# Halves of 64 rows in the first three steps of a gated attention and maxout kernel, and w_out eight rows to a partition

## The chip, the cores and the metric

The kernel runs on one core of a Trainium2 chip. The metric is the device time of one execution in microseconds. A core has TensorE (matmul; its weight loads are shown apart, as PEld), VectorE (DVE), ScalarE (ACT), GpSimd (POOL), SyncE (SP), and 16 DMA engines that the queues share. [...]

## The reference

Eight sequences of 3072 tokens go through attention without softmax, gated by u, and then through a layer that takes the larger of two projections:

```python
scores = (1.0 / S) * np.matmul(z, z.transpose(0, 2, 1))     # z: 8 x 3072 x 64
attn = np.maximum(scores, 0.0) ** 2
x = (u * np.matmul(attn, v)).reshape(B * S, D)              # u, v: 8 x 3072 x 256
g = np.maximum(x @ w1, x @ w2)                              # w1, w2: 256 x 1024
out = g @ w_out                                             # w_out: 1024 x 256
```

## The kernel before

A step is 512 tokens of one sequence (a group of four blocks of 128): 8 sequences of 6 steps, 48 steps. In step n a tile of scores (two blocks of rows by the 512 tokens) is a pair of products over 64 rows, one on each half of the array; relu takes it out of PSUM into a_sb, square makes it attn. Scores are symmetric, so a tile is computed once and turned by a transposing DMA on SyncE's queue (aT) for the step that needs the other side.

Attention times v goes two ways. From step 3 on a fast scheme with seven products in place of eight is used: halves of 64 rows and 256 columns named Xa, Xb, Ya, Yb, with sums on VectorE (es) and folded values of v (lf). The first three steps (PLAIN = 3) multiply plainly: a product of v's block over all 128 rows into each of two banks, acc0 and acc1, for each of the 24 blocks of rows (add_plain, L859). A first or last part of such a step takes four blocks for one bank and then for the other, so that a bank comes free early.

The second layer runs two to three steps behind. The maximum is computed as x(w1 - w2) through relu plus x w2 w_out, so w2 is transposed on TensorE once (w2t, L1593) and multiplied by w_out (w2o). The first-layer products are named d, in four units of two blocks of 512 columns; each unit has a first part a and a second part b (a0 b0 a1 a2 b1 b2 a3 b3), in which the two halves of the array work on different banks and then change over. The w_out products use the seven-product scheme too in steps 3 to 46; their four parts are s0 to s3 here. In a step the order is s0 a0 s1 b0 Xa s2 Xb a1 a2 s3 b1 b2 Ya (a3 in it) b3 Yb.

Where two parts change over between halves and banks, a fence keeps them apart: an empty instruction on GpSimd's queue waits for the last product before (mark, L93), and the next product waits for it (fence, L87). POOL's queue also issues the loads of v, u, z and the weights; a timed load waits for a product of TensorE (load, L106).

The order of TensorE's work is written out: a list of work with planned times, into which groups of score tiles ("windows", L1400) are laid at certain spots (L1461 to L1475). Everything else (which of ScalarE and VectorE does a tile, the order of each queue, which buffer a tile takes) is dealt by a planner that runs the list through costs and due times (find_orders, L1779) and keeps the best of 24 rounds. The DMA dictionary (L206) and FIRST_LOADS (L209) are its guesses of transfers; at_step(b, s, us) names the job of TensorE at a planned time in a step, and fixes when a load is requested.

The weights of the second layer come in with these layouts (L1580): w1 and w2 as "(c p) f -> p c f", w_out as "(c p) d -> p c d", row c x 128 + p of w_out in partition p, 1024 pieces of one row.

Of the kernel before, what the change touches and what calls it, by code (L numbers as in the profile page):

```python
# [11 lines left out]
def kernel(  # L12
# [45 lines left out]
    W2O_AT, A3_AT = 0, 4  # L58
# [47 lines left out]
    def load(timed=False, **kw):  # L106
        dma = pin(nc.gpsimd.dma_start(**kw))
# [98 lines left out]
    DMA = dict(turn=1180, uT=1130, zT=4220, store=1940, v=1680, u=1680, z=3130, w1=4100, w2=3000, wo=4500)  # L206
    DMA_SMALL, DMA_PART, DMA_FULL, DMA_FULL_TO = 970, 0.9, 1.1, 100000
    DMA_START, DMA_END, DMA_LATE, DMA_AHEAD, SP_ISSUE = {"SP": 870, "POOL": 1770}, 1330, 4000, 4500, 1450
    FIRST_LOADS = {("v", 0, 0): 0, ("v", 0, 1): 1200, ("v", 0, 2): 2500, ("v", 0, 3): 3700, ("v", 0, 4): 4900, ("v", 0, 5): 7700, ("u", 0): 6300}  # L209
# [209 lines left out]
    def add_pair(st, k0, head=None):  # L419
# [19 lines left out]
        def do_square(eng):  # L439
# [4 lines left out]
            RELU,  # L444
# [414 lines left out]
    def add_plain(st, keyed, ks, dcs):  # L859
        first = [st.count[dc] == 0 for dc in dcs]  # L860
        counts = []
        for k in ks:
            counts.append(st.count[dcs[0]])
            for dc in dcs:
                st.count[dc] += 1
        accs = [(f"acc{dc}", st.n) for dc in dcs]
        new = [a for a, f in zip(accs, first) if f]
        for pool, key in new:
            acc_buf(int(pool[-1]), key)

        def fn(_):
            for k, n in zip(ks, counts):
                for dc in dcs:
# [3 lines left out]
                        a_rows(st, k - k % 2)[:, k % 2],  # L877
# [5 lines left out]
        key = ("plain", st.n, keyed)  # L883
        for g in groups:
# [3 lines left out]
            {"PE": PE512 * len(ks) * len(dcs)},  # L888
# [184 lines left out]
    def add_second(st, split):  # L1073
# [17 lines left out]
        for i in range(KF // 2):  # L1091
# [23 lines left out]
            def halves_of(part, i=i, bank=bank):  # L1115
                if part:
                    fence.append(marks.pop(("d", n, i)))
                for kc in range(KD):
                    for half in range(2):
# [4 lines left out]
                            w1_sb[:, kc, ts(2 * i + j, P)],  # L1124
# [180 lines left out]
    plain_todo = []  # L1305

    for n, st in enumerate(steps):
# [57 lines left out]
        def put_plain(ks, dcs, reads):  # L1365
            global_i = len(plain_todo)
            i = sum(t[0] is st for t in plain_todo)
            plain_todo.append((st, i, ks, dcs))
            put(PE512 * len(ks) * len(dcs), False, ("plain", st.n, i), reads)

        for i, k0 in enumerate(own):
            if i in ((0, 1) if n else ()) + (len(own) - 2, len(own) - 1):
                if i in (0, len(own) - 2):
                    ks = [own[i], own[i] + 1, own[i + 1], own[i + 1] + 1]
                    for dc in range(KD):
                        put_plain(ks, [dc], [((n, own[i]), lat), ((n, own[i + 1]), lat)])
                continue
            for k in (k0, k0 + 1):
                put_plain([k], range(KD), [((n, k0), lat)])
# [21 lines left out]
    for i, (n, k0) in enumerate(tiles):  # L1401
# [13 lines left out]
        if tiles[i + 1 : i + 2] and tiles[i + 1][0] // NG > n // NG:  # L1415
            room = 0

# [43 lines left out]
    spots = [i for i, at in enumerate(begins) if free(i) and apart(at) and not work[i][1]]  # L1461
# [3 lines left out]
    for w in reversed(range(len(windows))):  # L1465
        limit = min([limit] + [due[r] for r in windows[w] if r in due])
        found = [i for i in spots if begins[i] <= limit]
        i = found[-1] if found else 0
# [4 lines left out]
    laid = {i: [w for w in ws if w > 6] for i, ws in laid.items()}  # L1473
    for w, i in ((2, 2), (3, 5), (4, 8), (5, 11), (6, 14)):
# [84 lines left out]
    for n in range(len(steps)):  # L1559
# [91 lines left out]
    for args in plain_todo:  # L1651
        st, i, ks, dcs = args
        add_plain(st, i, ks, list(dcs))
# [59 lines left out]
    for key, before in zip(pe_order, [None] + pe_order):  # L1713
        if key[0] == "score" and (before is None or before[0] == "plain"):
# [288 lines left out]
```

## Time and profile before

| | |
|---|---|
| median of 3 runs | 893.06 us (890.72 to 893.35) |
| profiled execution | 893.2 us, span 891.4 us, mean granted clock 0.998 |
| TensorE busy | 882.7 us of the span (99%) |
| VectorE, ScalarE busy | 802.4 us (90%), 757.9 us (85%) |
| GpSimd busy | 59.8 us (7%) |
| packets' time in SyncE's DMA queue (hardware), in GpSimd's (software) | 79.3% and 23.3% of the 16 engines' span |
| steps 0, 1, 2 on TensorE | products from 7.69 us, from 23.82, from 37.60; w2t at 50.45 |

The span is the time from the first to the last instruction of the profiled execution; the rest of its time lies around it. A busy TensorE is not one at its peak: matmuls are pipelined, their ends are modelled, and a gap of 0.1 us between two kinds of product does not show as idle. In the views a row gives the start, the length of the whole group, engine, line, operation, tiles, and the count; the idle time before it and what ended it stand in brackets.

### The profile page before, as it was taken

How to read it: one execution, taken by the hardware profiler on the slowest of the kernel's cores; microseconds unless marked ns; L12 is line 12 of the kernel's file. 1: busy time of each engine (PE TensorE's matmuls, PEld its weight loads, DVE VectorE, ACT ScalarE, POOL GpSimd, SP SyncE). 2: the span in 40 equal slices, each digit the busy share in tenths (PEclk: the TensorE clock that was granted, in tenths of full speed). 3: DMA queues.
4: the chain of work that ended last, by engine and by line, in shares of the span. 5: the costliest groups of instructions: out<-in, count | busy, mean ns of one | idle time of the engine just before them, and what ended most of it. 6: DMA issues, size and time to landing. Idle time of an engine off the chain costs nothing.

```text
span 891.4 us, 37531 instructions
## 1 busy us (share of the span) xinstructions
PE 882.7 (99%) x16501; PEld 738.0 (83%) x16501; DVE 802.4 (90%) x1720; ACT 757.9 (85%) x952; POOL 59.8 (7%) x127
## 2 busy tenths in 40 slices
PE   9999999999999999999999999999999999999998
PEld 3368888878889988888888878888888898888886
DVE  6867799989999999999999999989998999989985
ACT  8867998879988999789997899978999799997634
POOL 3100000000000000000000000000000010000000
PEclk9999999999999999999999999999999999999999
DMA  9999999999999989999899999999999999996722
GB/s 160 171 167 148 188 199 160 179 188 187 157 163 169 193 151 174 170 179 203 121 169 173 191 184 143 169 166 213 150 148 172 187 199 158 136 199 115 128 58 73
DMA packets 380853, 146.17 MB, mean 164 GB/s; under 512 B 359184, under 2 KB 360848, under 8 KB 380688
## 3 DMA queue, kind: packets, MB, share of 16 engines
q1 hardware_dynamic: 364128, 114.01, 79.3%
q0 software_dynamic: 16560, 29.74, 23.3%
q8 instruction: 129, 2.11, 1.0%
q14 instruction: 36, 0.29, 0.1%
HBM read 59.77 MB, written 25.17 MB: 95 GB/s over the span
## 4 chain that ended last, share of the span: by engine, by line
PE 93%; ACT 3%; DMA 1%; DVE 1%; issue 1%; POOL 0%
PE acc L86 48%; PE s_ps L86 46%; ACT a_sb L282 1%; DMA aT<-a_sb 1%; ACT g_sb L282 1%; ACT o_sb L282 0%; DMA o_sb<-in_z_dram 0%; ACT g_last L282 0%; DVE gs L299 0%; DVE gs L296 0%; ACT a_sb L288 0%; ACT w2T_sb L293 0%; PE w2t_ps L1593 0%; DVE e L296 0%; DVE a_sb L290 0%
## 5 line engine op out<-in xcount | busy, mean ns | idle before, releaser
L86 PEld LDWEIGHTS <-v_sb 64*128 64x128 bf16 (+1 forms) x4464 | 332.4, 94 | 62.2 <-issue 8.4
L282 ACT ACTIVATE a_sb<-s_ps 128x1024 bf16<-128x1024 f32 (+1 forms) x335 | 302.3, 941 | 36.5 <-PE s_ps L86 33.6
L86 PEld LDWEIGHTS <-lf 64*128 64x128 bf16 x3240 | 264.2, 94 | 16.2 <-POOLq L94 3.2
L86 PE MATMUL acc<-es,v_sb 64*128 64x256 bf16 x2160 | 274.9, 269 | 0.0
L86 PE MATMUL acc<-es,lf 64*128 64x256 bf16 x1080 | 245.0, 269 | 0.0
L86 PE MATMUL acc<-a_sb,lf 64*128 64x256 bf16 x1224 | 232.1, 269 | 0.0
L86 PE MATMUL s_ps<-xT,w_sb 64*128 64x512 bf16 (+1 forms) x1504 | 212.6, 376 | 0.1
L288 ACT ACTIVATE a_sb<-a_sb 128x1024 bf16<-128x1024 bf16 (+1 forms) x224 | 209.9, 966 | 1.5
L282 ACT ACTIVATE g_sb<-s_ps 128x1024 bf16<-128x1024 f32 x187 | 186.0, 1024 | 14.0 <-PE s_ps L86 12.0
L86 PE MATMUL acc<-aT,lf 64*128 64x256 bf16 x936 | 177.5, 269 | 2.0 <-DMA aT<-a_sb 2.0
L86 PE MATMUL acc<-a_sb,v_sb 64*128 64x256 bf16 (+1 forms) x1344 | 140.2, 279 | 0.4 <-DVE xT L303 0.2
L86 PE MATMUL s_ps<-zT 64*128 64x512 bf16 (+2 forms) x774 | 120.2, 334 | 1.0 <-DVE zT L130 0.4
L86 PEld LDWEIGHTS <-gs 64*128 64x128 bf16 x2816 | 103.3, 94 | 9.9 <-issue 0.7
L296 DVE TENSOR_TENSOR es<-aT 128x1536 bf16<-128x1536 bf16 (+1 forms) x117 | 106.2, 931 | 0.5
L86 PEld LDWEIGHTS <-w_sb 64*128 64x128 bf16 (+1 forms) x1520 | 78.2, 94 | 25.5 <-POOLq L94 1.5
L86 PEld LDWEIGHTS <-g_sb 64*128 64x128 bf16 x2304 | 87.7, 94 | 10.4 <-POOLq L94 7.3
L290 DVE TENSOR_TENSOR a_sb<-a_sb 128x1024 bf16<-128x1024 bf16 (+1 forms) x112 | 72.2, 648 | 22.7 <-ACT a_sb L282 22.6
L86 PE MATMUL acc<-aT,v_sb 64*128 64x256 bf16 x936 | 86.8, 270 | 0.0
L299 DVE TENSOR_TENSOR es<-a_sb 128x512 bf16<-128x512 bf16 x198 | 79.4, 419 | 8.2 <-PE acc L86 8.0
L86 PE MATMUL s_ps<-wf_sb,gs 64*128 64x128 bf16 x2112 | 85.6, 217 | 0.0
L296 DVE TENSOR_TENSOR es<-a_sb 128x1024 bf16<-128x1024 bf16 x108 | 72.7, 684 | 0.0
L86 PE MATMUL s_ps<-w_out_sb,g_sb 64*128 64x128 bf16 (+1 forms) x1600 | 72.6, 222 | 0.0
(94 smaller groups left out, 1101.4 us busy)
## 6 DMA issues: line engine op xcount, KB each, us to landing
out_dram<-o_sb SPq DMA_DIRECT2D x47, 512.0 KB, 4.9
v_sb<-in_v_dram POOLq DMA_DIRECT2D x48, 256.0 KB, 5.8
u_sb<-in_u_dram POOLq DMA_DIRECT2D x48, 256.0 KB, 5.0
aT<-a_sb SPq DMA_TRANSPOSE x228, 5.1
z_sb<-in_z_dram POOLq DMA_DIRECT2D x7, 384.0 KB, 6.3
w_sb<-in_moe_w_dram POOLq DMA_DIRECT2D x2, 512.0 KB, 6.7
uT<-u_sb SPq DMA_TRANSPOSE x48, 5.2
a_sb<-a_sb SPq DMA_TRANSPOSE x45, 5.6
```

Of the source, the lines that this page charges most:

```text
L86: newest[0] = pin(nc.tensor.matmul(*args, **kw)).ins
L282: pin(nc.scalar.activation(out_ap, in_ap, AF.Relu))
L288: pin(nc.scalar.activation(ap, ap, AF.Square))
L290: pin(nc.vector.tensor_mul(ap, ap, ap))
L296: pin(nc.vector.tensor_add(*args))
L299: pin(nc.vector.tensor_sub(*args))
```

## The change

In step 0 all but the last two tiles' products, and in steps 1 and 2 those of tiles 3 to 8 of 12, are made of half-row products: in mode A the lower half of v's block goes to acc0 while the upper half of it, for the other 128 columns, goes to acc1; in mode B the two change over. Six runs of step 0 alternate between the modes; steps 1 and 2 have one run of A and one of B between full products (mode F). At each change of mode there is a fence. The score windows of step 1 and the first of step 2 are grouped anew, and laid between the runs. The planner no longer counts a passage for scores beside halves.

w_out is read as "(p c) d -> p c d", eight rows in one piece for each partition. Row 8 p + c now lies in partition p, so the first layer takes every eighth column of w1 and w2 as a block: by_place gives that view, and it is used in the weights of all d products and in w2's transposes. The request times of some loads, guesses of DMA times and the order of two first loads (u of step 0 before the last two groups of v) change with it.

```diff
-    W2O_AT, A3_AT = 0, 4
+    W2O_AT, A3_AT = 1, 4
...
+    def by_place(tile_sb):
+        return tile_sb.rearrange("p c (q n) -> p c n q", n=KF)
...
-    DMA = dict(..., wo=4500)
+    DMA = dict(..., wo=3000)
-    FIRST_LOADS = {..., ("v", 0, 4): 4900, ("v", 0, 5): 7700, ("u", 0): 6300}
+    FIRST_LOADS = {..., ("v", 0, 4): 6300, ("v", 0, 5): 7700, ("u", 0): 4900, ("uT", 0): 12000}
...
-            RELU,
+            {"DVE": RELU["DVE"]} if (n, k0) == (1, 6) else RELU,
...
-    def add_plain(st, keyed, ks, dcs):
+    def add_plain(st, keyed, ks, dcs, mode):
...
-                st.count[dc] += 1
+                st.count[dc] += 1 if mode in "AB" else 2
...
+        key = ("plain", st.n, keyed)
+        before, after = (plain_modes.get(("plain", st.n, keyed + i)) for i in (-1, 1))
+        waits, marked = before not in (None, mode), after not in (None, mode)
 
         def fn(_):
+            if waits:
+                fence.append(marks.pop(("plain", st.n)))
             for k, n in zip(ks, counts):
+                moving = a_rows(st, k - k % 2)[:, k % 2]
+                if mode in "AB":
+                    for half in range(2):
+                        dc = half ^ "AB".index(mode)
+                        halved(
+                            half,
+                            tile_of(f"acc{dc}", st.n),
+                            v_tile(st.b, k // G)[:, k % G, ts(dc, P)],
+                            moving,
+                            start=n == 0,
+                            stop=n == 2 * NSB - 1,
+                        )
+                    continue
                 for dc in dcs:
                     matmul(
...
-                        stop=(n == NSB - 1),
+                        stop=(n == 2 * NSB - 2),
                     )
+            if marked:
+                marks["plain", st.n] = mark()
...
-                            w1_sb[:, kc, ts(2 * i + j, P)],
+                            by_place(w1_sb)[:, kc, 2 * i + j, :],
...
+    FIRST_RUNS = [("A", 0, 2), ("B", 0, 3), ("A", 2, 5), ("B", 3, 6), ("A", 5, 10), ("B", 6, 10)]
...
+        if n == 0:
+            for run in FIRST_RUNS:
+                first_windows.append(len(work))
+                put_halves(*run)
+            first_windows.append(len(work))
+            put_banks(10)
+        else:
+            put_banks(0)
+            put_whole(2)
+            put_halves("A", 3, 9)
+            put_halves("B", 3, 9)
+            put_whole(9)
+            put_banks(10)
...
+    windows[6:11] = [[(1, k0) for k0 in ks] for ks in ((0, 2), (4, 6, 8), (10, 12, 14), (16, 18, 20), (22,))] + [[(2, 0), (2, 2)], [(2, 4)]]
...
-    laid = {i: [w for w in ws if w > 6] for i, ws in laid.items()}
-    for w, i in ((2, 2), (3, 5), (4, 8), (5, 11), (6, 14)):
+    laid = {i: [w for w in ws if w > 7] for i, ws in laid.items()}
+    laid = {i: [w for w in ws if w not in (9, 10, 11, 12)] for i, ws in laid.items()}
+    for w, i in [*zip(range(2, 8), first_windows[1:]), (9, first_windows[-1] + 6), (10, first_windows[-1] + 8), (11, first_windows[-1] + 12), (12, first_windows[-1] + 15)]:
...
-            add_u(n, quiet(at_step(pb, ps, 2 if pb == 0 and ps < LAG else 1), ("Xa",)))
+            add_u(n, quiet(at_step(pb, ps, (2 if ps == 0 else 2.3) if pb == 0 and ps < LAG else 1), ("Xa",)))
...
-            v_at = [(0, 8), (3, 9), (4, 4), (4, 9), (5, 4), (5, 9)]
+            v_at = [(0, 8.7), (3, 9), (4, 4), (4, 9), (5, 4), (5, 9)]
...
-        (lambda: tile_of(*W2), moe_w2, "w2", (0, 7), W2, "(c p) f -> p c f"),
-        (lambda: w1_sb, moe_w1, "w1", (1, 2), None, "(c p) f -> p c f"),
-        (lambda: w_out_sb, moe_w_out, "wo", (2, 2), None, "(c p) d -> p c d"),
+        (lambda: tile_of(*W2), moe_w2, "w2", (0, 6.9), W2, "(c p) f -> p c f"),
+        (lambda: w1_sb, moe_w1, "w1", (1, 2.3), None, "(c p) f -> p c f"),
+        (lambda: w_out_sb, moe_w_out, "wo", (2, 2.3), None, "(p c) d -> p c d"),
...
-                pin(nc.tensor.transpose(tile_of("mm", ("w2t", 0))[:, dc, nb, :], tile_of(*W2)[:, dc, ts(nb, P)], ident))
+                pin(nc.tensor.transpose(tile_of("mm", ("w2t", 0))[:, dc, nb, :], by_place(tile_of(*W2))[:, dc, nb, :], ident))
...
-        if key[0] == "score" and (before is None or before[0] == "plain"):
+        if key[0] == "score" and (before is None or plain_modes.get(before) == "F"):
             jobs[key].ways = {"PE": jobs[key].ways["PE"] + 2 * SWITCH}
...
-                j.done = dma_free[0] + (DMA_LATE if begin > 125000 and j.key[0] != "zT" else DMA_END)
+                j.done = dma_free[0] + (DMA_LATE + 1500 * (j.key[0] == "v") if begin > 125000 and j.key[0] != "zT" else DMA_END)
...
-    early_loads = [("v", 0, g) for g in range(NG - 1)] + [("u", 0), ("v", 0, NG - 1)]
+    early_loads = [("v", 0, g) for g in range(NG - 2)] + [("u", 0), ("v", 0, NG - 2), ("v", 0, NG - 1)]
```

More of the change, by code (lines that the diff above doesn't have):

```diff
@@ L887, in add_plain @@
             key,
-            {"PE": PE512 * len(ks) * len(dcs)},
+            {"PE": PE512 * len(ks) * len(dcs) // (2 if mode in "AB" else 1)},
             fn,
@@ L1123, in halves_of @@
                             bank(j),
-                            w1_sb[:, kc, ts(2 * i + j, P)],
+                            by_place(w1_sb)[:, kc, 2 * i + j, :],
                             tile_of(*xT)[:, :, kc, :],
@@ L1363, with put_plain, rows_at, put_halves @@
         n_plain = 0
-        def put_plain(ks, dcs, reads):
-            global_i = len(plain_todo)
+        def put_plain(mode, ks, dcs, reads):
             i = sum(t[0] is st for t in plain_todo)
[L1368 to L1379, printed above, removed]
+            plain_todo.append((st, i, ks, dcs, mode))
+            plain_modes["plain", st.n, i] = mode
+            ns = PE512 * len(ks) * len(dcs) // (2 if mode in "AB" else 1)
+            put(ns, False, ("plain", st.n, i), reads)
+        def rows_at(i):
+            return [((n, own[i]), lat)]
+        def put_halves(mode, first, end):
+            for i in range(first, end):
+                put_plain(mode, [own[i], own[i] + 1], range(KD), rows_at(i))
+        def put_whole(i):
+            for k in (own[i], own[i] + 1):
+                put_plain("F", [k], range(KD), rows_at(i))
+        def put_banks(i):
+            ks = [own[i], own[i] + 1, own[i + 1], own[i + 1] + 1]
+            for dc in range(KD):
+                put_plain("F", ks, [dc], rows_at(i) + rows_at(i + 1))
+        if n == 0:
[11 more added lines that the diff above has]
+            put_banks(10)
     assert LAG == 3
@@ L1459, in apart @@
         return n >= LAG or (at - starts[n]) % (6 * 432) == 0
-    spots = [i for i, at in enumerate(begins) if free(i) and apart(at) and not work[i][1]]
+    spots = [i for i, at in enumerate(begins) if free(i) and apart(at) and not work[i][1] and at >= starts[1]]
     GAP_FIRST, GAP, GAP_LATER = 2100, 600, 1200
@@ L1651 @@
     for args in plain_todo:
-        st, i, ks, dcs = args
-        add_plain(st, i, ks, list(dcs))
+        st, i, ks, dcs, mode = args
+        add_plain(st, i, ks, list(dcs), mode)
     for b in range(B):
```

11 lines of the change are left out of this document (5 added, 6 removed).

## The prediction

> **What bounds the kernel now.** First the page: which engine is busy, and what the chain that ended last consists of.
>
> ```profile
> PE 882.7 (99%) x16501; PEld 738.0 (83%) x16501; DVE 802.4 (90%) x1720; ACT 757.9 (85%) x952; POOL 59.8 (7%) x127
> PE 93%; ACT 3%; DMA 1%; DVE 1%; issue 1%; POOL 0%
> ```
>
> TensorE is busy 882.7 of 891.4 us and makes 93% of the chain. So an edit pays in two ways only: TensorE's own work gets shorter, or one of the few gaps of TensorE closes. The view of the waits, for TensorE, names one gap of weight, and the chain in order of time gives its place and what it costs.
>
> ```profile
> PE acc L86 <- DMA aT<-a_sb: 2.0, 1, 2.0
> ```
> ```profile
> 131.31 2.12 PE s_ps L86 x64
> 182.68 8.27 DMA aT<-a_sb
> 242.81 2.12 PE s_ps L86 x64
> 350.71 2.12 PE s_ps L86 x64
> 458.42 2.12 PE s_ps L86 x64
> ```
>
> The same place of the loop comes round every six steps. From 242.81 to 350.71 it takes 107.9 us, to 458.42 another 107.7; but from 131.31 to 242.81 it takes 111.5. That one round loses 3.7 us, and in it lies the only step of the chain that is a transfer: a transposing DMA into aT, issued at 182.68, on which TensorE waits until about 190.95. The wait is 2.0 us, so 1.7 us of the 3.7 are something else. The busy time by short stretches (columns: stretch, length, then busy time of PE, PEld, DVE, ACT, POOL, then PEclk, DMA share, GB/s) shows what:
>
> ```profile
> 190.00:192.00 2.00, 1.01 (x20) 0.91 (x21) 2.00 (x4) 0.47 (x1) 0.00 (x0) 0.94 0.99 194
> 192.00:194.00 2.00, 2.00 (x40) 1.97 (x37) 1.96 (x5) 1.61 (x2) 0.00 (x0) 0.50 1.23 265
> 194.00:196.00 2.00, 2.00 (x28) 1.66 (x26) 0.00 (x0) 1.01 (x2) 0.53 (x1) 0.70 1.67 340
> ```
>
> Behind the wait the granted clock is 0.94, 0.50 and 0.70: 2 x (0.06 + 0.50 + 0.30) = 1.7 us of full-speed work lost. So this one late transfer costs 2.0 + 1.7 = 3.7 us. [...]
>
> Why is that transfer late? SyncE's queue at the same place of two rounds:
>
> ```profile
> 153.48 13.19 SPq L103 DMA_TRANSPOSE aT<-a_sb  x6
> 182.68 5.71 SPq L103 DMA_TRANSPOSE aT<-a_sb  x2
> 257.53 15.23 SPq L103 DMA_TRANSPOSE aT<-a_sb  x6
> 288.60 4.15 SPq L103 DMA_TRANSPOSE aT<-a_sb  x2
> ```
>
> The places lie 111.5 us apart on TensorE. 257.53 - 111.5 = 146.0, so the first round issues its six transposes 7.5 us later than the second one; at 288.60 - 111.5 = 177.1 it is still 5.6 us late. It is a backlog, and it is being worked off. It began where the DMA engines went from idle to full; the busy tenths of the DMA engines in the stretch 38 to 52 us (40 slices of 0.35 us), and then in 50 to 190:
>
> ```profile
> DMA  0000000499947938999999999999999999999962
> ```
> ```profile
> DMA  9999999989999989999999999999999999999999
> ```
>
> Idle from 38 to 40.5, busy ever after, up to the wait. The w_out load is the first of that flood.
>
> **The change part by part.** *Halves.* A pair of half-row products, one on each half of the array, takes the place of one full product; there are as many pairs as there were products, so the streaming itself gains nothing. What goes is the cost of passing between full-row products and score products, which are halves already. TensorE's rows in step 1:
>
> ```profile
> 26.50 0.82 PE L86 MATMUL s_ps<-zT 64*128 64x512 bf16 x6
> 27.25 2.76 PE L86 MATMUL acc<-a_sb,v_sb 128*128 128x512 bf16 x12
> 29.95 0.82 PE L86 MATMUL s_ps<-zT 64*128 64x512 bf16 x6
> ```
>
> One period is 29.95 - 26.50 = 3.45 us. Twelve products, at (2.76 - 0.38) / 11 = 0.216 each, are 2.59; six score halves, two at a time, are 0.65. The rest, 0.21 us, is two passages: 0.105 each. Before the change there are 14 groups of scores among products, 6 in step 0 and 4 each in steps 1 and 2, so 28 passages. In the changed order I count: step 0 runs in halves up to its last two tiles, which leaves 1 passage; step 1 has a group at its start (2), one where halves begin (1), one where they end (1), and the rest stand among halves; step 2 the same 4. That is 9. W2O_AT = 1 moves the full-row w2o products behind the first group of step 3's halves, 2 more. 28 - 11 = 17 passages, 1.8 us gained.
>
> Against it stands the beginning of step 0:
>
> ```profile
> 7.69 1.02 PE L86 MATMUL acc<-a_sb,v_sb 128*128 128x512 bf16 x4
> 8.39 1.28 DVE L290 TENSOR_TENSOR a_sb<-a_sb 128x1024 bf16<-128x1024 bf16 x2
> 8.65 0.61 PE L86 MATMUL s_ps<-zT 64*128 64x512 bf16 x4
> 9.18 0.11 PEld L86 LDWEIGHTS <-v_sb 128*128 128x128 bf16 x2 [0.42 <-issue]
> ```
>
> Now four full products (0.86) and a group of scores lie between 7.69 and 9.18, and the square of the second tile, the first of VectorE's two from 8.39, is ready about 9.05. In mode A the first tile gives only 0.43 us of products, and the scores come behind the second tile: TensorE is out of work at 8.12 and waits until about 9.15, 1.0 us. Step 3 thus starts about 1.8 - 1.0 = 0.8 us earlier. ScalarE's relus of step 0 get their scores up to 0.9 us later at first; by my dealing none of the later groups waits for them. If that cover is gone, 0.9 us is the price.
>
> *Fences.* Each change of mode is a wait of TensorE on a GpSimd instruction that itself waits for the last product before: 6 in step 0, 3 in each of steps 1 and 2. An existing fence, with the loads of the weights around it:
>
> ```profile
> 185.44 0.24 PE L86 MATMUL s_ps<-xf_sb,xT 64*128 64x128 bf16 x2
> 185.45 0.17 PEld L86 LDWEIGHTS <-w_sb 64*128 64x128 bf16 x4
> 185.50 0.61 PE L86 MATMUL s_ps<-xT,w_sb 64*128 64x512 bf16 x4
> 185.79 0.37 PEld L86 LDWEIGHTS <-g_sb 64*128 64x128 bf16 x8 [0.17 <-POOLq L94]
> 185.93 0.40 PE L86 MATMUL s_ps<-w_out_sb,g_sb 64*128 64x128 bf16 x8
> 186.16 0.28 PEld L86 LDWEIGHTS <-g_sb 64*128 64x128 bf16 x8
> 186.21 0.40 PE L86 MATMUL s_ps<-w_out_sb,g_sb 64*128 64x128 bf16 x8
> ```
>
> The last product ends at 185.68 and the fenced weights load at 185.79: 0.11 us, hidden behind four halves (0.43 us). In the changed order two or three tiles' scores (0.43 to 0.65 us) stand in every such place; a product's tail of 0.16 beyond its slot, 0.11 and the load's lead of about 0.1 make 0.37. I take nothing, margin 0.06. Behind the fence on GpSimd's queue only its load issues wait; the moved times (6.9, 8.7, 2.3) place each load after a fence, not ahead of it. A load issue in front would cost up to its own length:
>
> ```profile
> 40.67 0.92 POOL L107 DMA_DIRECT2D w_out_sb<-in_moe_w_out_dram  x1 [12.55 <-PE acc L86]
> ```
>
> Seven loads lie in these steps, so 0 to 6 us; I take 0.
>
> *Loads.* The w_out load goes from 1024 pieces of a row to 128 of eight rows. Time from issue to landing:
>
> ```profile
> w_sb<-in_moe_w_dram POOLq DMA_DIRECT2D x2, 512.0 KB, 6.7
> w_out_sb<-in_moe_w_out_dram POOLq DMA_DIRECT2D x1, 512.0 KB, 8.5
> ```
>
> The nearest row for the same bytes in larger pieces is w_sb's 6.7: up to 1.8 us less of a full queue, or nothing; I take 0.9. It is requested 0.4 us later in the step, which starts 0.8 earlier. So the flood ends 0.4 + 0.9 = 1.3 us earlier, and TensorE reaches the late aT 0.8 us earlier: the wait of 2.0 becomes about 1.5, bounds 0.6 to 2.4. The dealing of all later work is computed anew, so this transfer may also stand elsewhere in its queue; the rounds behind show no wait at all.
>
> *w1 by place.* All first-layer products now take weights whose columns lie eight elements apart, 1504 matmuls, and the 16 transposes of w2 as well. No row of this trace has such a load. Cost from below 0, from above in the rival. I take 0, because the nearest row, w_sb's 4 loads in 0.17, leaves room: (0.17 - 0.09) / 3 = 27 ns each, 54 ns for the two of a pair that streams 216.
>
> **The sum.** The profiled execution took 893.2 us (its span 891.4 and 1.8 around it), 0.1 over the median of 893.06. Less 0.8 for steps 0 to 2. If the wait is gone: less 3.7 more, 888.7. If it is still 1.5 but too short for the clock to drop: the flood's end decides, 893.2 - 1.3 - 1.7 = 890.2. My forecast is between, **889.5 us**.
>
> **The rivals.** *The wait stays and drops the clock.* Then only the flood's end counts: 893.2 - 1.3 = 891.9, or 893.2 if w_out's form saves nothing and the first part's gain is all given back as waiting. For it: the backlog is DMA's, and 2.0 us of wait has once been enough. Against: the dealing is new. The runs before, 890.72 to 893.35, spread by 2.6 us, less than the 3.7 of wait and drop together but more than the drop alone, so it may not come each time.
>
> *Slower: the spaced weights load slowly.* Where products of 128 columns run, eight and the two of xT behind them, five pairs, go from 185.93 to 186.21: 56 ns a pair, hardly more than its two loads take (eight in 0.28: (0.28 - 0.09) / 7 = 27 ns each, 54 a pair). If a spaced load took twice as long, the two would take 107 ns, and the first pair behind such a stream would start its second half 107 - 54 = 53 ns late, in three places of a step: a0 behind s0, b0 behind s1, b1 behind s3. 3 x 44 steps x 53 ns = 7.0 us: 893.2 - 3.7 + 7.0 = 896.5, or 899.4 with the wait staying. It decides from 27 ns upward; at four times (107 ns each) the three places lose 160 ns, 21 us, and beyond that the pairs of 512 columns themselves. The row that would be spaced:
>
> ```profile
> L86 PEld LDWEIGHTS <-w_sb x1520: 92/94/98, 51.3 to 880.2; 64*128 64x128 bf16 x188, 128*128 128x128 bf16 x2
> ```
>
> [...] No row of before can settle this.
>
> *A new wait.* The new dealing puts another operand late, once, with the clock's drop: 893.2 - 0.8 + 3.7 = 896.1 if the old wait stays too, 892.4 if it only moves. *The halves don't run side by side*: spoken against by the score halves above, six in three slots.
>
> **How the numbers follow.** Forecast 0.50; the wait stays (or only moves) 0.30; spaced weights 0.13; a second wait 0.07. A measurement of this kernel tells about 0.3%, 2.7 us, from no change, so faster means under 890.4 and slower over 895.7. The forecast is nearly all below 890.4, the wait that stays lies in between, the last two above: faster 0.48, same 0.33, slower 0.19. The range goes from 887.5 (the wait gone, w_out's full 1.8, some of the passages' margin) to 896.5, which takes in a second wait and the lower price of spaced weights. The first two cases alone hold 887.5 to 893.5.
>
> **What would show it.** Right: 0.43 us of products at 7.7, a wait of 1.0, then score rows without a gap of 0.1 on each side up to the last tiles of step 0; w2t's transposes about 0.8 us before 50.4; no row of PE waiting on aT, or one under 1.5 us, with the clock at 1.00 in every stretch; the first round at 107.8 us. Wrong: LDWEIGHTS of w_sb over 100 ns, or gaps at the first product of a first-layer unit in every round, which would lift the later rounds above 107.7; PE waiting on GpSimd's queue in the first 50 us; a clock of 0.50 anywhere.

## The result, and the profile after

The changed kernel takes 898.15 us in the median of 12 executions (892.89 to 906.15), the kernel before 893.11 beside it (890.67 to 899.14): the ratio is 1.0060, 95% interval 1.0032 to 1.0087. (Here and below the ratios leave out executions more than 1.5% above the fastest of their kernel; the medians hold all.) The prediction of 889.5 us, and its range up to 896.5, missed: it is slower. The profiled execution took 903.62 us, its span 901.9; that of before 893.2.

The page after, its first line on the engines and the chain that ended last:

```profile
PE 885.6 (98%) x16589; PEld 765.5 (85%) x16589; DVE 801.3 (89%) x1720; ACT 758.5 (84%) x952; POOL 59.4 (7%) x127
PE 92%; DMA 3%; ACT 2%; DVE 2%; issue 1%; POOL 0%; SPq 0%; POOLq 0%; ACTq 0%; DVEq 0%
```

TensorE still bounds, but DMA's share of the chain has gone from 1% to 3%. The beginning came out as forecast. TensorE's rows of step 0, and a weight load behind a fence (columns: start, length, and in brackets the wait ahead of it):

```profile
7.84 0.59 PE L86 MATMUL acc<-a_sb,v_sb 64*128 64x512 bf16 x4
9.45 0.61 PE L86 MATMUL acc<-a_sb,v_sb 64*128 64x512 bf16 x4 [1.01 <-DVE a_sb L293]
10.31 0.61 PE L86 MATMUL acc<-a_sb,v_sb 64*128 64x512 bf16 x4
```
```profile
10.16 0.26 PEld L86 LDWEIGHTS <-v_sb 64*128 64x128 bf16 x4 [0.17 <-POOLq L94]
```
```profile
L1640 PE MATMUL w2t_ps<-ident,w_sb x16: 219/225/230, 49.1 to 50.0; 128*128 128x128 bf16 x16
```

Four half-row products take 0.59 to 0.61 us, where four over all rows took 1.02 at the same place in the kernel before: the two halves run side by side. The wait of 1.01 us is there. The weight load waits 0.17 us for the fence at 10.16, but the product it serves starts at 10.31 without a wait. From the first product of step 0 to w2's transposes it is 49.1 - 7.84 = 41.3 us, against 50.45 - 7.69 = 42.8 before: 1.5 us gained, where 0.8 was forecast. And no wait for aT is left at 189 us. But TensorE's waits now read:

```profile
PE acc L86 <- DMA aT<-a_sb: 3.4, 1, 3.4
PE acc L86 <- DMA a_sb<-a_sb: 1.7, 1, 1.7
PE acc L86 <- DVE a_sb L293: 1.0, 1, 1.0
```

The first two stand in step 3, a few microseconds after the gained 1.5. TensorE's rows there, and the busy time in stretches of 2 us with the granted clock (the number after POOL's):

```profile
57.25 0.38 PE L86 MATMUL acc<-aT,v_sb 64*128 64x256 bf16 x4
61.07 0.29 PE L86 MATMUL acc<-aT,lf 64*128 64x256 bf16 x2 [3.43 <-DMA aT<-a_sb]
63.11 0.58 PE L86 MATMUL acc<-a_sb,v_sb 64*128 64x256 bf16 x3 [1.67 <-DMA a_sb<-a_sb]
```
```profile
62.00:64.00 2.00, 0.89 (x10) 0.72 (x11) 2.00 (x5) 0.00 (x0) 0.00 (x0) 0.50 0.97 78
64.00:66.00 2.00, 2.00 (x22) 1.61 (x20) 1.93 (x6) 0.00 (x0) 0.00 (x0) 0.50 1.27 167
68.00:70.00 2.00, 2.00 (x33) 1.83 (x31) 0.36 (x2) 0.36 (x1) 0.00 (x0) 0.81 0.96 104
```

Two waits, and half clock from 61.93 us for 6.83 us by the trace's record of the clock, so it begins within the second wait. Adding 3.43 + 1.67 + 3.4 = 8.5 us counts a part of that wait twice. Measured between equal places of TensorE, against the run zearly_after below, which has the same order and no stop, it costs 8.3 us (72.88 against 64.32, less the 0.30 by which it was later already). The two profiled executions differ by 10.4 us: 8.3 from here, less 1.5 at the start, less the 3.7 of the old gap at 189 us, and 3.4 from the rounds of six steps, each of which takes 0.45 us longer (below). Of the 3.9 left, 1.4 are waits for ScalarE and VectorE in the round behind the stop, 1.3 are waits for nothing visible (at 313 and 381 us), and 1.2 stay unassigned.

One wait in one profile isn't a median. The mean granted clock of each execution tells how often clock is lost, though not where: 0.998 means about 3.6 us at half clock (0.002 x 2 x 893). Of 24 executions of the changed kernel (12, and 12 in a second run) 13 show 0.998 or less, with a median of 902.4 us; the other 11 have a median of 896.8. Of 145 executions of the kernel before, run beside the kernels below, 28 show it (median 898.5), and the other 117 have a median of 893.3. I call them **executions with lost clock** below. In the changed kernel they are more frequent, 54% against 19%, and its other executions are slower too, by 3.5 us; the rounds less the gain at the start explain 1.9 of these.

### The profile page after: what moved, and what is told of

It is laid out like the page before. It is cut to its first block, busy times and chain, and to the rows that moved or that the text cites. A ratio compares the mean times of both kernels' runs of the same rounds, so it can differ in the third digit from the quotient of the medians.

```text
span 901.9 us, 37712 instructions
## 1 busy us (share of the span) xinstructions
PE 885.6 (98%) x16589; PEld 765.5 (85%) x16589; DVE 801.3 (89%) x1720; ACT 758.5 (84%) x952; POOL 59.4 (7%) x127
## 4 chain that ended last, share of the span: by engine, by line
PE 92%; DMA 3%; ACT 2%; DVE 2%; issue 1%; POOL 0%; SPq 0%; POOLq 0%; ACTq 0%; DVEq 0%
PE acc L86 47%; PE s_ps L86 44%; DMA a_sb<-a_sb 2%; ACT g_sb L285 1%; DMA z_sb<-in_z_dram 1%; DMA aT<-a_sb 0%; ACT a_sb L285 0%; ACT a_sb L291 0%; DVE es L299 0%; DVE a_sb L293 0%; DVE es L302 0%; DVE o_sb L299 0%; DVE zT L133 0%; DVE gs L302 0%; DVE e L299 0%
## 5 line engine op out<-in xcount | busy, mean ns | idle before, releaser
L86 PEld LDWEIGHTS <-v_sb 64*128 64x128 bf16 x4552 | 334.6, 94 | 61.5 <-issue 10.0
L86 PE MATMUL s_ps<-xT,w_sb 64*128 64x512 bf16 (+1 forms) x1504 | 215.9, 378 | 0.5 <-ACT g_sb L285 0.4
L291 ACT ACTIVATE a_sb<-a_sb 128x1024 bf16<-128x1024 bf16 x225 | 210.9, 966 | 1.5
L86 PE MATMUL acc<-a_sb,v_sb 64*128 64x256 bf16 (+2 forms) x1424 | 142.0, 284 | 3.9 <-DMA a_sb<-a_sb 1.7
L86 PE MATMUL s_ps<-zT 64*128 64x512 bf16 (+2 forms) x774 | 122.4, 333 | 1.8 <-ACT o_sb L296 0.7
L86 PEld LDWEIGHTS <-w_sb 64*128 64x128 bf16 (+1 forms) x1520 | 105.8, 142 | 14.0 <-issue 1.2
L86 PEld LDWEIGHTS <-g_sb 64*128 64x128 bf16 x2304 | 91.1, 95 | 8.5
L86 PE MATMUL s_ps<-w_out_sb,g_sb 64*128 64x128 bf16 (+1 forms) x1600 | 76.8, 226 | 0.0
```

Source lines behind the costliest of these rows:

```text
L86: newest[0] = pin(nc.tensor.matmul(*args, **kw)).ins
L291: pin(nc.scalar.activation(ap, ap, AF.Square))
```

## Which part of the change: the parts alone

*The spaced weights and the layout of w_out, without halves.* Edits to the kernel before; layout_only has both lines, spaced_only the first (its rows of w_out then meet other columns of the first layer, so it computes another sum by the same instructions):

```diff
-    w1_sb[:, kc, ts(2 * i + j, P)]
+    by_place(w1_sb)[:, kc, 2 * i + j, :]      # and in w2's transposes
-    (lambda: w_out_sb, moe_w_out, "wo", (2, 2), None, "(c p) d -> p c d"),
+    (lambda: w_out_sb, moe_w_out, "wo", (2, 2), None, "(p c) d -> p c d"),
```

> The kernel before with the spaced weights of w1 and w2 alone (w_out's rows then meet other columns of the first layer than in the reference); no halves, w_out in pieces of one row, the order as before. Theory S: weights loads of w_sb 141 ns, 108.2 us a round, so 893.1 + 2.9 = 896. If the round's longer time came from the halves' dealing instead: 107.8 us a round and 893.1.

> The kernel before with w_out in eight rows to a partition and the spaced weights; no halves, the order as before. Theory S: 896 less what the wide load brings in the backlog, up to 1.3 us: 894.7 to 896. Theory W: the wide pieces hold up the turns, a wait on a transfer between 50 and 65 us or a longer one at 189: 897 to 900.

*The halves, without the spaced weights.* Edits to the changed kernel: contiguous columns in by_place, and for halves_only also the old layout of w_out, so that halves_wide keeps its wide rows (and computes another sum too):

```diff
-    return tile_sb.rearrange("p c (q n) -> p c n q", n=KF)
+    return tile_sb.rearrange("p c (n q) -> p c n q", n=KF)
```

> The changed kernel with w_out read as before (one row to a piece) and contiguous weights of w1 and w2; halves, score windows, request times and the whole dealing stay. Theory S (spaced weights cost in every round, the halves' schedule makes the early waits): the round of six steps comes back from 108.2 to 107.8 us, weights loads of w_sb 94 ns, w2t at about 49.1 us, and the waits on transfers between 50 and 65 us stay in some executions: median about 895 (898.15 less 2.9). Theory W (the wide pieces of w_out hold up the turning transfers in the DMA engines): the early waits are gone too, and the median is 889 to 891.

> The changed kernel with contiguous weights of w1 and w2 (each partition's rows of w_out then meet other columns of the first layer than in the reference); w_out still in 128 pieces of eight rows. Beside the changed kernel it takes away the spaced loads alone. Theory S: 108.2 to 107.8 us a round, 2.9 us less in all, about 895, early waits as in the changed kernel. Theory W: the same 2.9 us less, early waits as in the changed kernel; against halves_only it is slower by the early waits, 3 to 6 us.

Measured (12 executions each, ratio to before with its interval):

| kernel | median us | ratio | with lost clock | clean round of six steps |
|---|---|---|---|---|
| spaced_only | 894.24 | 1.0021 (0.9993 to 1.0049) | 3 | 107.83 |
| layout_only | 895.06 | 1.0012 (0.9982 to 1.0041) | 3 | 107.83 |
| halves_only | 901.36 | 1.0050 (1.0019 to 1.0080) | 10 | 108.05 |
| halves_wide | 895.21 | 1.0021 (0.9989 to 1.0053) | 3 | 108.05 |

A clean round is the time between two equal places of TensorE six steps apart, with no wait in it; before it is 107.71, in the changed kernel 108.16. So the spaced weights cost 0.12 us a round, 0.9 us over 7.5 rounds, and the other 0.33, 2.5 us, come with the rest of the change, though no halves are left after step 2. Theory S, which put all of it down to the weights, is out. The load that was in dispute:

```profile
L86 PEld LDWEIGHTS <-w_sb x1520: 137/141/168, 50.0 to 890.2; 64*128 64x128 bf16 x188, 128*128 128x128 bf16 x2
```

141 ns against 94: half as much again, nearly all of it behind running products. halves_only, with w_out in 1024 pieces, stops in step 3 as well (1.3 us for aT, 0.9 for a_sb<-a_sb): the wide rows are not what holds the turnings up, and theory W is out too. halves_only and halves_wide differ in w_out's layout alone and lose clock in 10 and in 3 of 12 executions; no run shows why, and a share of twelve executions is a coarse number.

## What holds up the turnings of step 3: the load of z

SyncE's queue at that place, and the load of the next sequence's z on GpSimd's queue; then z's time from issue to landing, after and before:

```profile
39.60 8.48 SPq L103 DMA_TRANSPOSE aT<-a_sb  x3
48.18 1.50 SPq L103 DMA_TRANSPOSE a_sb<-a_sb  x1
```
```profile
45.17 0.53 POOL L107 DMA_DIRECT2D z_sb<-in_z_dram  x1 [3.64 <-ACT a_sb L285]
```
```profile
DMA to landing us min/median/max: 15.8/15.8/15.8
```
```profile
DMA to landing us min/median/max: 9.7/9.7/9.7
```

z is requested at 45.17 and lands at 60.97. The third of the three turnings of aT, requested at 42.33, lands at 61.02, and that of a_sb at 63.06, as the chain in order of time has it:

```profile
48.18 14.88 DMA a_sb<-a_sb
```

In the kernel before the turning of a_sb is issued at 46.21 and takes 10.2 us, so it lands at 56.4, and z at 56.2:

```profile
46.21 1.21 SPq L103 DMA_TRANSPOSE a_sb<-a_sb  x1
```

In the changed kernel TensorE goes on at 61.07 and 63.11. While they are under way the DMA engines are busy but move 60 GB/s, against 154 before; the row of 50 to 60 us (last numbers: DMA share, GB/s), before and after:

```profile
50.00:60.00 10.00, 9.90 (x105) 6.73 (x105) 9.68 (x25) 6.71 (x9) 0.53 (x1) 1.00 1.36 154
```
```profile
50.00:60.00 10.00, 7.54 (x65) 5.04 (x64) 2.93 (x7) 5.46 (x8) 0.53 (x1) 1.00 1.28 60
```

The trace shows that both kinds slow down together: z, with 15.8 us against 9.7 in the kernel before, and the third turning land within 0.05 us, and the turnings' packets of 256 bytes that begin between 50 and 58 us take 135 ns in the mean, against 32 in the kernel before.

*z later,* in the changed kernel, in halves_only and in the kernel before:

```diff
-    z_at, zT_at = (2, 6), (3, 2)
+    z_at, zT_at = (3, 6), (4, 2)
```

> The changed kernel with the second sequence's z requested one step later (behind the load of u of step 4, about 63 instead of 45 us; its turning moved from step 3 to step 4). Theory Z (the turns that step 3 reads share the DMA engines with z's load and land only when it does): no wait on a transfer between 50 and 65 us, the transfers in 50 to 60 us back to about 150 GB/s, median 893 to 895 instead of 898.15. Theory Q (the halves' order brings one turn more into the queue by 42 us, and the queue is late whatever is beside it): the wait stays, 897 to 899.

> halves_only (w_out in pieces of one row, contiguous weights) with z requested one step later. Theory Z: the waits between 50 and 65 us go, median 892 to 894 instead of 901.4, and faster than the same kernel with the other layout by the 0.9 us of the spaced weights. Theory Q: 899 to 901.

> The kernel before with z requested one step later. It has no wait at 50 to 65 us to lose, but its later backlog shrinks or not: theory Z gives no change there, 893 to 894, or the wait at 189 us goes in more executions, 891 to 893; a z load that disturbs the turns at 63 us instead would show as waits at 65 to 80 us, 895 and more.

Measured: 903.65, 905.94 and 906.57 us (ratios 1.0114, 1.0132, 1.0143; 6, 5 and 4 executions). The wait of step 3 is gone in zlate_after and zlate_halves, as theory Z says (the first d product of step 1 comes at 64.1 us in zlate_after, 72.6 in the changed kernel); zlate_before had none to lose. In all three another wait has come, from about 80 us on, where step 6 needs zT; in zlate_after:

```profile
PE s_ps L86 <- DMA zT<-z_sb: 8.0, 1, 8.0
```

The move was too far, and each kernel is slower for it, where 3 to 9 us less, or no change in the kernel before, were expected.

*z earlier,* in the place of one load of v (in the kernel before 8 stands for 8.7):

```diff
-    z_at, zT_at = (2, 6), (3, 2)
-    v_at = [(0, 8.7), (3, 9), (4, 4), (4, 9), (5, 4), (5, 9)]
+    z_at, zT_at = (0, 8.7), (3, 2)
+    v_at = [(3, 6), (3, 9), (4, 4), (4, 9), (5, 4), (5, 9)]
```

> The changed kernel with contiguous weight loads and the old w_out layout; the request for the second sequence's z moves from about 45 us (step 2) to about 22 us (step 0), in the place of one v request, which moves to step 3. Theory Z (the z load shares the DMA engines with the turnings and u/uT loads that step 3's d products read, so that all land only when z lands, at about 61 us): with z landed before 40 us, the turn of aT that is requested at about 42 us lands within 10 us instead of 18.7, no transfer wait over 1 us between 50 and 70 us and none for zT at 80 us, no stretch of granted clock 0.5 there; bytes moved at 50 to 60 us at 120 GB/s or more; profiled span about 888 to 890 us, time 890 to 892. Theory Q (the early waits come from the order in which the turnings are requested: one turn more stands in the queue at 42 us, whatever else is loaded): the aT wait of 1 to 3 us at 57 to 61 us stays, 892 to 896.

> The changed kernel whole, with z asked for at about 22 us instead of 45, as in the run with contiguous weights. Theory Z: the waits of 3.4 and 1.7 us and the half clock from 61.9 us for 6.8 us go, about 3.4 + 1.7 + 3.4 = 8.5 us in the profiled execution; what is left of the change is the gain ahead of w2's transposes of 1.5 us, the gap of before at 189 us (3.7 us) if it is gone, less 0.45 us a round of six steps (0.33 dealing, 0.12 spaced weights) over 7.5 rounds, 3.4 us: time 891 to 893. Theory Q: the waits stay, 896 to 900.

> The kernel before with z asked for at about 22 us instead of 46, in the place of one v request. It tells whether the gap at 189 us and the early shares of DMA belong to the load of z at all. Theory Z: z shared the engines with the turnings there too but landed by 56 us, ahead of their use, so there is little to gain: same within 0.3%, 891 to 893; the wait at 189 us stays (it depends on requests made long after) or goes by chance of the backlog. Theory Q: no change either, within 0.3%.

Measured: zearly_halves 895.45 us (ratio 1.0015, 0.9985 to 1.0044), zearly_after 900.16 (1.0034, 0.9999 to 1.0068), zearly_before 895.76 (1.0035, 1.0001 to 1.0068). No wait in step 3 in any of the three profiles and none for zT; 50 to 60 us in zearly_after:

```profile
50.00:60.00 10.00, 9.90 (x112) 7.34 (x112) 9.76 (x27) 5.33 (x7) 0.53 (x1) 1.00 1.02 176
```

The profiled execution of zearly_after took 892.34 us, 11.3 less than that of the changed kernel. But the medians did not follow: 7 of 12 executions still lose clock, and 6 of 12 in each of the other two, zearly_before too. So the wait was taken away and the frequency was not. zearly_before is the warning here: neither it nor the kernel before has a wait in step 3, and with z moved it loses clock in 6 of 12, against 5 of 35 of the kernel before beside it. Moving z, and a load of v to step 3 in exchange, may cost clock of its own, so these runs can't tell how much of the changed kernel's lost clock goes with z. To see more executions, I ran both once more, unchanged:

> The changed kernel once more, for a second profile and for twelve more executions with their granted clocks. Theory T (the loss comes from executions in which step 3 waits for its turnings at about 57 to 63 us and the clock then halves): about half of the executions show a granted clock of 0.998 or less, with a median near 901.5, the others near 894; if the profiled execution is one of the disturbed, the wait for aT or a_sb lies between 50 and 70 us. Rival L (waits anywhere, by chance): the same share, but the profile of a disturbed execution shows its wait elsewhere, as a wait for nothing visible or for a transfer after 70 us.

> The changed kernel with z asked for at about 22 us once more. Theory Z (the load of z is what holds up step 3's turnings): no transfer wait between 50 and 70 us in the profile; if this execution is disturbed, its wait lies elsewhere (a wait for nothing visible, or a transfer later), and so the disturbed share stays at about half. Rival: the wait at 50 to 70 us is there again, then z is not what holds the turnings up.

after_again: 900.17 us (ratio 1.0059, 1.0033 to 1.0084), 6 of 12 with lost clock; zearly_again: 896.96 (1.0029, 1.0005 to 1.0053), 3 of 12. The profiled execution of after_again lost no clock, but the same place stops, for less:

```profile
58.61 0.38 PE L86 MATMUL acc<-a_sb,v_sb 64*128 64x256 bf16 x3 [0.96 <-DMA a_sb<-a_sb]
```
```profile
50.00:60.00 10.00, 8.95 (x91) 6.34 (x90) 7.59 (x20) 5.33 (x7) 0.53 (x1) 1.00 1.21 89
```

zearly_again again has none. Over all profiles with z requested at about 45 us: in seven (the four without halves, step0_halves, and late_out and steps12_out below) z landed after 7.2 to 10.7 us, and step 3 did not wait; in the six others, all with halves in steps 1 and 2, z took 12.4 to 17.4 us, and five of them stopped there, for 0.4 to 8.1 us. **Shown:** with z out of the way, later or earlier, step 3 waits in none of seven profiles, five of them with halves in steps 1 and 2, and with z in the way it waits only where z lands late. **Not shown:** why that load is slow in some executions and not in others (all six slow ones have the line of the planner treated below, late_out and steps12_out lack it, step0_halves has it too; whether it has a part in this was not tried), and where the executions of the z-early kernels lose their clock: 10 of 24 of zearly_after and zearly_again do, against 13 of 24, a difference that such numbers can't tell. One profile of that kind is zearly_halves (898.95 us, clock 0.998):

```profile
306.54 0.23 PE L86 MATMUL s_ps<-wf_sb,gs 64*128 64x128 bf16 x2 [3.29 <-issue]
```

TensorE stands for 3.29 us and waits for nothing that the profile shows.

## Which steps' halves

Edits to halves_only: step0_halves leaves steps 1 and 2 in full products, with step 1's tiles grouped as before; steps12_halves does so with step 0.

```diff
-            put_whole(2)
-            put_halves("A", 3, 9)
-            put_halves("B", 3, 9)
-            put_whole(9)
+            for i in range(2, 10): put_whole(i)          # step0_halves
...
-            for run in FIRST_RUNS:
-                first_windows.append(len(work))
-                put_halves(*run)
+            for i in range(10): put_whole(i)             # steps12_halves
```

> halves_only with halves in step 0 alone: steps 1 and 2 in full products, score tiles of step 1 grouped by three as before; w_out and weights as before. By the passages counted, 0.1 us is lost or gained in step 0 against the kernel before (1.2 us of passages less 1.0 us of waiting). Theory Q: the turns are queued about as in the kernel before and the early waits are gone, 893 to 895. If it is step 0's later first scores that make the turns late: 898 to 901 as in halves_only.

> The changed kernel with contiguous weight loads and the old w_out layout, and step 0 in full products of before; only steps 1 and 2 have their v products as halves (steps' passages go from 28 to fewer, those of step 0 stay, and the 1.0 us wait at the start goes). It is the counterpart of the run with halves in step 0 alone, which had no transfer wait between 50 and 70 us. If the halves of steps 1 and 2 with the re-dealt score tiles of step 1 make the d part of step 3 come before its turnings have landed: transfer wait of 1 to 3 us there and 893 to 897. If it takes both (step 0 earlier and steps 1 and 2): no such wait, 890 to 893.

step0_halves: 895.80 us (1.0028, 0.9994 to 1.0063), 4 of 12 with lost clock, no wait in step 3. steps12_halves: 893.35 (1.0012, 0.9979 to 1.0046), 3 of 12; its profiled execution, at 902.38, is one of the three and stops in step 3 for 4.64 and 3.42 us, while the other nine have a median of 893.06. Both have rounds of 108.04 to 108.05 us, so neither the re-dealt tiles of step 1 (which step0_halves lacks) nor step 0's halves make the loss of 0.33 us a round. The two also tell where the 1.5 us of the beginning come from: from the first product of v to w2's transposes step0_halves takes 42.75 us, the kernel before 42.76, and steps12_halves 41.31. The halves of step 0 gain nothing there; those of steps 1 and 2, with their re-dealt tiles, gain all of it.

## Where 0.33 us a round come from: one line of the planner

In the later steps TensorE's instructions come in the same order before and after; VectorE's do not. TensorE falls behind at three places of a round, by 0.08 to 0.14 us each. One of them, at VectorE and TensorE, before:

```profile
560.99 0.42 DVE L299 TENSOR_TENSOR lf<-v_sb,lf 128x512 bf16<-128x512 bf16 x1
```
```profile
561.57 0.27 PE L86 MATMUL acc<-es,v_sb 64*128 64x256 bf16 x1
561.59 0.27 PE L86 MATMUL acc<-es,lf 64*128 64x256 bf16 x1
```

And after:

```profile
569.87 0.42 DVE L302 TENSOR_TENSOR v_sb<-v_sb 128x512 bf16<-128x512 bf16 x1
570.21 0.42 DVE L302 TENSOR_TENSOR lf<-v_sb,lf 128x512 bf16<-128x512 bf16 x1
```
```profile
570.46 0.27 PE L86 MATMUL acc<-es,v_sb 64*128 64x256 bf16 x1
570.68 0.28 PE L86 MATMUL acc<-es,lf 64*128 64x256 bf16 x1
```

VectorE now does the last fold of v (v_sb) ahead of the one that TensorE waits for (lf). Before, lf is done at 561.41 and its product starts 0.02 us behind its partner; after, lf is done at 570.63 and the product starts 0.22 us behind. First I took it for the planner's luck, which keeps one of 24 rounds of planning. before_14 gives the kernel before another plan, and seed_wide gives halves_wide the due-time margins that the planner of before had ended with:

```diff
-    ROUNDS = 24
+    ROUNDS = 14                                  # before_14
-    margin, best_end = {}, None
+    margin, best_end = {("Ya", 12, 0): 2830.0, ...}, None     # seed_wide, 48 entries
```

> The kernel before, with the planner stopped after 14 of its 24 rounds of planning, so that it keeps another plan: TensorE's order of steps is the same, VectorE's and ScalarE's standing order in each six steps another. Theory P (the 0.33 us a round that the changed kernel loses come from the planner's choice of that standing order): the undisturbed rounds of six steps are not 107.71 us but differ by 0.1 to 0.6 us, and the undisturbed executions by 0.7 to 4.5 us (892.5 to 897.5). Rival D (the re-dealt tiles or halves themselves cost it): the rounds stay at 107.71 within 0.05, undisturbed executions at 893.2.

> The changed kernel with contiguous weight loads (w_out eight rows to a partition, another sum) and, for steps 6 and later, the due-time margins that the planner of before had gathered for its choice (48 entries). VectorE's standing order comes nearer to that of before. Theory P: undisturbed rounds of six steps 107.70 to 107.85 us instead of 108.03, so that the earlier start stays as a gain: undisturbed executions at 891.5 to 892.5. Rival D: rounds stay at 108.03, undisturbed executions at 893.5 to 894.5. The share of disturbed executions is as with halves in all three steps, a half, in either case.

before_14: 893.62 us (1.0002, 0.9975 to 1.0029), rounds of 107.79: another plan costs 0.08, not 0.1 to 0.6. seed_wide: 899.18 (1.0026, 0.9994 to 1.0057), rounds of 108.13: the margins bring nothing. Both are against theory P as it was put. The diff has a line that is not about halves at all: it lets the planner reckon each load of v 1.5 us later. Taken out of the changed kernel, and out of steps12_halves:

```diff
-    j.done = dma_free[0] + (DMA_LATE + 1500 * (j.key[0] == "v") if begin > 125000 and j.key[0] != "zT" else DMA_END)
+    j.done = dma_free[0] + (DMA_LATE if begin > 125000 and j.key[0] != "zT" else DMA_END)
```

Without it the orders of VectorE, ScalarE and SyncE in the later steps are those of before, instruction by instruction.

> The changed kernel without the one line by which the planner reckons the loads of v 1.5 us later. Theory V (that line sets the standing order of VectorE, in which fold 3 of v runs ahead of the fold 2 that TensorE waits for, and so the loss of 0.33 us a round): undisturbed rounds of six steps 107.83 us (107.71 and 0.12 of the spaced weights) instead of 108.16; undisturbed executions 0.33 x 7.5 = 2.5 us shorter, near 892 instead of 894.3. Rival D (the halves and their fences, or the re-dealt tiles, cost it): rounds stay at 108.16. The share of disturbed executions is near a half in either case, so that the median says little: 893 to 898.

> Halves in steps 1 and 2 only, contiguous weight loads, the old w_out layout, and without the line on the loads of v. Theory V: undisturbed rounds of six steps 107.71 us instead of 108.05; undisturbed executions 893.06 - 2.5 = 890.6 us; with about a quarter of the executions disturbed, as in the same version with the line, a median of 890.5 to 892, which is below the kernel before. Rival D: rounds at 108.05, median 893 to 894.

Equal places of the chain of waits, one round apart, in the changed kernel, in late_out and in steps12_out:

```profile
485.47 2.56 PE s_ps L86 x68
593.64 2.56 PE s_ps L86 x68
```
```profile
476.27 2.56 PE s_ps L86 x68
584.10 2.56 PE s_ps L86 x68
```
```profile
455.65 2.12 PE s_ps L86 x64
563.35 2.12 PE s_ps L86 x64
```

108.17, 107.83 and 107.70 us: to 0.01 what was expected. So the line costs 0.33 us a round, 2.5 us in all, and it does so through the planner's order of VectorE: the order was the cause after all, only not by the choice among 24 rounds. late_out takes 895.34 us (1.0028, 0.9994 to 1.0061; 5 of 12 with lost clock, the others 893.78 where about 892 was expected). **steps12_out takes 891.50 us** (889.45 to 905.94; ratio 0.9976, 0.9952 to 1.0000), 3 of 12 with lost clock, the others 891.38 where 890.6 was expected. The median lies in the range expected, and it is the only version that came out below both kernels, 0.24% below the kernel before; but the interval ends at no difference, so that it is faster is not shown. Of the change it keeps the halves of steps 1 and 2, the tiles dealt anew for them and the request times.

## Why the prediction was wrong

The medians differ by 5.0 us, and 3.6 of gain were forecast. The rounds (3.4 us) less the gain at the start (1.5) make 1.9 of the 5.0. The other 3.1 go with the stops and the lost clock; the profiles show those of step 3, and where the rest lies stays open.

- **The gap at 189 us** was the main term (3.7 us of gain) and the first step that failed. It was real in the profiled execution, but it is no property of the kernel: by its granted clock of 0.998 that execution is of the kind of which there are 28 in 145. Neither spaced_only nor layout_only, whose instructions stand in the same order, waits for aT there, nor do zearly_before and before_14. What most executions of before don't lose, the change can't give back to them.
- **The rival "a new wait"** was right in kind, with a chance of 0.07 and without a place. The sum knew that DMA was full from 40.5 us on; it looked only at what the flood's end does at 189 us, not at who else waits inside it. Coming 1.5 us earlier to step 3 takes 1.5 us off the margin there; the larger part of the stop is that the turning of a_sb landed at 63.06 us where it had landed at 56.4 before. The rival was priced at 3.7 us, and the stop cost 8.3 in the profiled execution.
- **"The dealing of all later work is computed anew"** was written down and given no price. It cost 2.5 us, through a line that stood in the diff and was not weighed. The statement that later rounds would go on at 107.8 is where it failed.
- **Spaced weights**: taken at 0, priced at 7.0 us in the rival; 0.9 measured. The load went from 94 to 141 ns, so it is slower, as the rival said, but its rule (the two loads of a pair are the pace) gave too much, 0.16 us a step where 0.02 was measured: the loads are mostly covered. The rival's 896.5 also leaves out the 0.8 us that the sum had taken off; by its own terms it is 895.7.
- **Right:** 1.0 us of wait at the start (1.01), fences at no cost (no product waits for one in the first 50 us), w_out's wide load (7.2 us against 8.5; 0 to 1.8 forecast, 0.9 taken). The passages of steps 1 and 2 were undersized: start to w2's transposes gained 1.5 where 0.8 was summed, and by steps12_halves 1.45 of it come from steps 1 and 2, where eight passages at 0.105 make 0.84; the 0.15 summed for step 0 did not come.

## What to carry to other kernels

A gap in one profile is a term of the sum only if it is in most executions: compare the granted clock or the lowest time of several runs first, for a time of 893.2 with a gap of 3.7 in it and others as long without it say that each execution loses something else. Here the share of the DMA engines was 1.17 at 40.5 to 50 us and 1.28 at 50 to 60, and TensorE, 1.5 us ahead, stood at step 3 until transfers landed at 61.02 and 63.06 us; so look up for each transfer behind a gain when it lands and how much it can spare. And in a kernel with a planner, read each changed cost as a change of its own: one guess of a landing cost 2.5 us, more than the 1.5 that the halves gained.

## What was not expected of the hardware

- A half clock does not follow from the length of a wait alone. In before, behind a wait of 1.97 us that ended at 190.99, the clock stood at 0.50 for 3.41 us from 191.77; in the changed kernel, behind a wait of 3.43 us and within one of 1.67, for 6.83 us from 61.93. In halves_only, with waits of 1.3 and 0.9 us in step 3, the clock of 60 to 70 us was 0.83. In after_again two waits of 2.1 us, one for VectorE and one for zT, left the mean clock of the whole execution at 1.000.
- The same load of z, requested at 45.1 us in late_out and at 45.2 in the changed kernel, took 7.9 us to land in the one and 15.8 in the other. In the changed kernel its 128 packets of 3 KB begin at 49 us and the last ends at 60.4. The median packet took 247 ns and the mean one 567, so most were quick: 31 of the 128 took over 600 ns. In the kernel before, where z landed after 9.7 us, the median is 247 ns too, the mean 471, and 26 took over 600.
- In the changed kernel the waits for nothing visible go with the queue whose kind the page calls "instruction" (q8, packets of 16 KB, one every 6.8 us in the mean). Between 10 and 880 us TensorE has four such waits of 0.15 us or more, the longest of 1.01 us, ending at 215.97, 222.17, 313.03 and 380.62 us, and each ends 1.3 to 1.6 us behind the end of one of these packets. Those four packets took 881 to 1185 ns, against a median of 974, and the slowest of the run, of 2094 ns (at 530.2), was followed by no such wait: a slow packet alone does not make one. No run changed that queue, so this is an association, not a test.
